# One-hot tiles of a routing table: two of six per batch moved from GpSimd to ScalarE

## The chip, the cores and the metric

The kernel runs on one core of a Trainium2 chip. The metric is the device time of one execution in microseconds (us). One execution was also profiled; its trace gives each instruction's start and length on TensorE (PE, with its weight loads as PEld), VectorE (DVE), ScalarE (ACT), GpSimd (POOL) and SyncE (SP, which issues DMAs).

## The reference

Four batches of 768 tokens, 8 heads of 64. First a chunked attention: each chunk of 32 queries sees 8 memory keys and a window of its neighbours. Its output, 3072 tokens of 512, goes to a top-1 mixture of 8 experts.

```python
def _moe_ref(x, modality_id, w_gate, modality_bias, w1, w2):
    logits = x @ w_gate + modality_bias[modality_id]
    e_idx = np.argmax(logits, axis=1)
    ...
    gate_w = probs[np.arange(N), e_idx]
    for e in range(E):
        mask = e_idx == e
        ...
        h = np.maximum(x[mask] @ w1[e], 0.0)
        out[mask] = gate_w[mask, None] * (h @ w2[e])
```

## The kernel before, in words

The attention is a loop over 32 half units (a unit is two heads of one batch, a half is 384 of its 768 tokens; variable `i`). One round of the loop issues: the score matmuls of half i (`scores`, line 339), the transposes and the exponential of half i-1 (`exps_t`, lines 357 on PE and 359 on ACT, tile `PT`), the maximum and the subtraction of half i on DVE (`less_max`, 347 and 350), then in even rounds the key transposes of the next unit and their copies (`trans_k`, `store_k`, line 331, three on ACT and one on DVE), in odd rounds Pool's copies of shared value rows (`share_v`, line 289) and the query transposes (`trans_q`, line 303; `store_q`, line 308 on ACT); then the second product of half i-1 (`attend`, line 369, which needs `PT`), the transposes of half i-2 (`trans_x`, line 391 on PE, copied by ACT in line 394) and the normalisation of half i-1 on DVE (`normalize`, lines 377 to 384).

When the four units of a batch are done, a generator `route(b)` finds each token's expert and its rank in the expert's list, and writes the token's number into a table, 128 rows by 192 columns. The table is built by six matmuls (line 663), one per 128 tokens: the stationary tile `l1` is a one-hot of the low part of the rank (128 wide, tile `l` in the trace), the moving tile `a1` is a one-hot of expert and high part times the token's number (192 wide, tile `a`). `lo` and `ac` are the numbers that the one-hots are made from; both are ready well before. The table of the first three batches is read by the first `gather` (line 720), which opens the expert stage.

The generator's steps are fed into the attention loop by `pump(k)`, which issues the next k steps, each of which ends with a `yield "v"`. There are calls of `pump` in each round: one after the maximum, one after the subtraction, three and three around `store_k` (the second three behind the three copies on ACT), three inside and after `normalize`, one at the round's end. The batch before the last takes three times as many.

Each engine runs its queue in order. PE, SP and Pool run in the order in which the program issues. ACT and DVE do so too, but only up to round 26 (`MAN = 26`); from there to the end of the attention a planner orders these two by its own costs. Batches 0 and 1 are routed before round 26, batch 2 around rounds 25 to 29, batch 3 behind the loop, where the expert stage already runs.

Of the kernel before, what the change touches and what calls it, by code (L numbers as in the profile page):

```python
# [15 lines left out]
ALU = mybir.AluOpType  # L16
# [4 lines left out]
P = 128  # L21
B, H, S, D = 4, 8, 768, 64
NMEM = 8
NCH = S // 32
NT = S // P
# [11 lines left out]
ROW_X = ROW_R1 + 1  # L37
ROW_L = 32
NEARLY = 3
NPOOL = 2  # L40
NP3 = 0
NACT = 2
CPOOL = (10, 12, 13, 14, 15)
MAN = 26
# [8 lines left out]
def tile_chunk_attention_top1_moe(  # L53
# [14 lines left out]
    nc = tc.nc  # L68
# [22 lines left out]
    def bank():  # L91
        return ps.tile([P, 512], F32, name="tr", tag="tr", bufs=4)
# [72 lines left out]
    iota = const.tile([P, 192], F32, name="iota")  # L165
# [4 lines left out]
    tokm = const.tile([P, N // P], F32, name="tokm")  # L170
# [352 lines left out]
    def route(b):  # L523
# [72 lines left out]
        lo = sm.tile([P, NT, 1], F32, name="lo")  # L596
        nc.vector.scalar_tensor_tensor(lo[:, :, 0], hi[:, :, 0], -float(P), rank[:, :, 0], op0=ALU.mult, op1=ALU.add)
        yield "v"
        ac = sm.tile([P, NT, 1], F32, name="ac")
# [39 lines left out]
        for t in range(NT):  # L639
            l1 = rt.tile([P, P], F32R, name="l1", bufs=NT)  # L640
            a1 = rt.tile([P, 192], F32R, name="a1", bufs=NT)
            T = b * NT + t
            if b == B - 1 and NP3 <= t < NP3 + NACT:
                dist = sm.tile([P, 192], F32, name="dist", bufs=2)
                nc.scalar.activation(dist[:, 0:P], iota[:, 0:P], AF.Abs, scale=-1.0, bias=lo[:, t])
                nc.scalar.activation(l1, dist[:, 0:P], AF.Relu, scale=-1.0, bias=1.0)
                dist = sm.tile([P, 192], F32, name="dist", bufs=2)
                nc.scalar.activation(dist, iota, AF.Abs, scale=-1.0, bias=ac[:, t])
                nc.scalar.activation(a1, dist, AF.Relu, scale=tokn[:, T:T + 1], bias=tokm[:, T:T + 1])
                hot.append((l1, a1))  # L650
                continue
            eng = nc.gpsimd if t < (NPOOL, NPOOL, NPOOL, NP3)[b] else nc.vector
            eng.tensor_scalar(l1, iota[:, 0:P], lo[:, t], None, op0=ALU.is_equal)
            yield "v"
            eng.tensor_scalar(a1, iota, ac[:, t], tokm[:, T:T + 1], op0=ALU.is_equal, op1=ALU.mult)
            yield "v"
            hot.append((l1, a1))
        if b == B - 1:
# [171 lines left out]
    t = bank()  # L830
# [23 lines left out]
    for i in range(n + 2):  # L854
# [53 lines left out]
        if i >= 2:  # L908
            u2, hf2 = units[i - 2]
            if hf2 == 1 and u2 % 4 == 3:  # L910
                routing.append((route(u2 // 4), True, u2 // 4, 0))
# [186 lines left out]
```

## Time and profile before

| | |
|---|---|
| timed runs | 453.59 us median of 3 (453.19 to 454.4) |
| profiled execution | 455.18 us, of which 453.4 us from first to last instruction |
| busy PE, DVE, ACT, POOL | 425.5, 310.5, 261.6, 195.8 us |
| mean granted TensorE clock | 0.984 of full |

The span falls in two stages: the attention up to about 145 us, and the expert stage behind it. An engine's busy share says little by itself; what counts is which wait ends last at a place. "Idle" in brackets in the rows is the time that an engine stood still before an instruction, with what released it.

### The profile page before, as it was taken

What the parts mean: (1) busy time and instruction counts of PE and PEld (TensorE: products, weight loads), DVE (VectorE), ACT (ScalarE), POOL (GpSimd) and SP (SyncE); (2) the same over time, 40 slices, a digit from 0 to 9 for tenths busy, and PEclk for the clock granted to TensorE, in tenths of its full rate; (3) what the DMA queues carried; (4) which work ended last, traced back from release to release, by engine and by line L of the source; (5) the groups of instructions that cost most, each with busy time, mean ns of one, the idle gap of its engine ahead of it and who ended that gap; (6) DMA issues with size and microseconds to landing.
All of it is one profiled execution on the core that took longest, in us unless ns stands there. A gap on an engine that the chain in (4) does not pass through costs nothing. (4 is left out here: it accounts for less than half of the span.)

```text
span 453.4 us, 11700 instructions
## 1 busy us (share of the span) xinstructions
PE 425.5 (94%) x4009; PEld 359.0 (79%) x4009; DVE 310.5 (68%) x746; ACT 261.6 (58%) x524; POOL 195.8 (43%) x373
## 2 busy tenths in 40 slices
PE   7879999999977998999999999999999999999993
PEld 4658787776856787989796977989898988898982
DVE  7888799797877699848465454757666574848430
ACT  5747776675636664747366455656565655657421
POOL 8867679579798932214051211303040404040201
PEclk9989999999979999999999999999999999999997
DMA  6899999999977502177196834202662201111101
GB/s 185 149 227 205 220 218 205 207 209 198 220 180 213 192 3 93 54 227 226 38 261 208 225 97 142 90 0 95 180 210 76 90 5 50 47 49 48 46 2 46
DMA packets 74818, 61.66 MB, mean 136 GB/s; under 512 B 36091, under 2 KB 64979, under 8 KB 74740
## 3 DMA queue, kind: packets, MB, share of 16 engines
q1 hardware_dynamic: 68000, 41.50, 40.2%
q0 software_dynamic: 5888, 19.11, 13.8%
q8 instruction: 36, 0.59, 0.6%
q14 instruction: 42, 0.34, 0.3%
q10 hardware_dynamic: 852, 0.11, 0.2%
HBM read 77.43 MB, written 12.76 MB: 199 GB/s over the span
## 5 line engine op out<-in xcount | busy, mean ns | idle before, releaser
L760 PEld LDWEIGHTS tr<-xt,w 128*128 128x128 f32 x1152 | 141.0, 189 | 4.9 <-issue 2.6
L760 PE MATMUL tr<-xt,w 128*128 128x256 f32 (+1 forms) x1152 | 142.9, 284 | 1.8 <-PEq L1059 0.6
L770 PE MATMUL av<-wh,h 128*128 128x512 f32 x384 | 128.4, 400 | 0.0
L795 POOL DMA_INDIRECT out_dram<-o,ix_now x24 | 24.2, 1008 | 157.1 <-ACT o L791 156.2
L764 DVE SCALAR_TENSOR_TENSOR h<-tr,h 128x256 fp32r<-128x256 f32 x96 | 40.6, 423 | 70.8 <-ACT h L761 53.1
L770 PEld LDWEIGHTS av<-wh,h 128*128 128x128 f32 x384 | 72.2, 188 | 17.3 <-issue 1.7
L770 PE MATMUL av<-wl,h 128*128 128x512 f32 x192 | 75.8, 395 | 0.0
L289 POOL COPY vw<-vw 24x384 f32<-24x384 f32 (+1 forms) x128 | 61.1, 515 | 24.5 <-DMA vw<-in_v_dram 23.2
L708 DVE TENSOR_TENSOR wl<-raw,wh 128x512 fp32r<-128x512 f32 x91 | 63.0, 692 | 8.1 <-ACT wh L706 0.8
L761 ACT ACTIVATE h<-tr 128x256 fp32r<-128x256 f32 x96 | 36.8, 385 | 51.8 <-PE tr L760 32.7
L708 DVE TENSOR_TENSOR w<-raw,w 128x512 fp32r<-128x512 f32 x93 | 60.4, 694 | 8.4 <-ACT w L706 8.4
L706 ACT CAST wh<-raw 128x512 fp32r<-128x512 f32 x96 | 58.8, 614 | 1.3 <-DMA raw<-in_moe_w_dram 1.3
L706 ACT CAST w<-raw 128x512 fp32r<-128x512 f32 x96 | 53.8, 622 | 0.0
L791 ACT ACTIVATE o<-av,gate_now 128x512 f32<-128x512 f32 x24 | 16.2, 689 | 46.3 <-PE av L770 37.3
L770 PEld LDWEIGHTS av<-wl,h 128*128 128x128 f32 x192 | 36.2, 188 | 7.1
L331 ACT COPY kbd<-tr 64x672 f32<-64x672 f32 x47 | 36.5, 777 | 6.4 <-PE tr L325 5.5
L369 PE MATMUL av<-vw,PT 128*32 128x130 f32 x768 | 29.3, 286 | 3.7 <-ACT PT L359 1.8
L359 ACT ACTIVATE PT<-tr 128x384 f32<-128x384 f32 x32 | 15.8, 492 | 28.6 <-PE tr L357 28.1
L339 PE MATMUL sc<-kbd,qT 128*32 128x128 f32 x768 | 29.3, 289 | 1.9 <-POOL kbd L313 1.9
L723 POOL DMA_INDIRECT xg<-xd,gx x24 | 26.5, 1105 | 9.8 <-POOL gx L721 6.2
L369 PEld LDWEIGHTS av<-vw,PT 128*32 128x32 f32 x768 | 20.5, 113 | 9.3 <-ACT PT L359 4.3
L743 ACT CAST xt<-tr 128x512 fp32r<-128x512 f32 x24 | 13.9, 586 | 23.0 <-PE tr L741 13.4
(237 smaller groups left out, 524.5 us busy)
## 6 DMA issues: line engine op xcount, KB each, us to landing
raw<-in_moe_w_dram SPq DMA_DIRECT2D x192, 256.0 KB
k<-in_k_dram SPq DMA_DIRECT2D x16, 384.0 KB
q<-in_q_dram SPq DMA_DIRECT2D x16, 384.0 KB
xd<-xb POOLq DMA_DIRECT2D x16, 384.0 KB, 6.0
vw<-in_v_dram SPq DMA_DIRECT2D x32, 184.0 KB
vw<-in_mem_v_dram SPq DMA_DIRECT2D x32, 48.0 KB
vw<-in_v_dram SPq DMA_DIRECT2D x32, 6.0 KB
vw<-in_v_dram SPq DMA_DIRECT2D x32, 2.0 KB
```

Of the source, the lines that this page charges most:

```text
L289: nc.gpsimd.tensor_copy(vw[r0:r0 + 24, c + 1:c + 1 + w, h, 0:D], vw[r0 + 32:r0 + 56, c:c + w, h, 0:D])
L331: copy(dst.rearrange("p c (i j) -> p c i j", j=2)[:, :, :, j], win)
L339: nc.tensor.matmul(sc[32 * j:32 * j + 32, t * P:(t + 1) * P], qT[:, 32 * c:32 * c + 32], kbd[:, c].rearrange("p h m -> p (h m)"), start=Tr ...
L369: nc.tensor.matmul(avb[32 * j:32 * j + 32, t * W:(t + 1) * W], PT[:, t * P + 32 * j:t * P + 32 * j + 32], vw[:, c].rearrange("p h d -> p ( ...
L706: nc.scalar.copy(wh[i], raw[i])
L708: (eng or nc.vector).tensor_sub(wl[i][:, s], raw[i][:, s], wh[i][:, s].bitcast(F32))
L723: nc.gpsimd.indirect_dma_start(out=xg[t], out_offset=None, in_=xd[0:rows], in_offset=bass.IndirectOffsetOnAxis(ap=gx[:, t:t + 1], axis=0))
L760: nc.tensor.matmul(pw, wt[f][:, c * P:(c + 1) * P], x[:, c, 0:w], start=(n == 0), stop=(n == 11))
L761: nc.scalar.activation(hh[:, f], ph, AF.Relu)
L764: nc.vector.scalar_tensor_tensor(hl[:, f], ph, 0.0, hh[:, f].bitcast(F32), op0=ALU.max, op1=ALU.subtract)
L770: nc.tensor.matmul(pos[t], x, w[8 + f], start=(f == 0 and n == 0), stop=(f == 7 and n == 2))
L795: nc.gpsimd.indirect_dma_start(out=out, out_offset=bass.IndirectOffsetOnAxis(ap=ix_now[:, t:t + 1], axis=0), in_=outs[t], in_offset=None, ...
```

## The change

Before, of the six pairs of one-hot tiles of each of the first three batches, the first two were made by Pool (two instructions a pair) and the last four by DVE. Now the first four are made by DVE and the last two by ACT, in the way that two pairs of the last batch were made already: the absolute distance to the wanted column, then a rectifier that leaves 1 (or the token's number) at distance 0 and 0 elsewhere, so four instructions a pair. Two `yield "v"` are put among those, so a pair counts two steps of the pump as the others do. In the last batch the same pairs stay on the same engines.

```diff
-NPOOL = 2
-NP3 = 0
 NACT = 2
...
-            if b == B - 1 and NP3 <= t < NP3 + NACT:
+            if (t < NACT) if b == B - 1 else (t >= NT - NACT):
                 dist = sm.tile([P, 192], F32, name="dist", bufs=2)
                 nc.scalar.activation(dist[:, 0:P], iota[:, 0:P], AF.Abs, scale=-1.0, bias=lo[:, t])
                 nc.scalar.activation(l1, dist[:, 0:P], AF.Relu, scale=-1.0, bias=1.0)
+                yield "v"
                 dist = sm.tile([P, 192], F32, name="dist", bufs=2)
                 nc.scalar.activation(dist, iota, AF.Abs, scale=-1.0, bias=ac[:, t])
                 nc.scalar.activation(a1, dist, AF.Relu, scale=tokn[:, T:T + 1], bias=tokm[:, T:T + 1])
+                yield "v"
                 hot.append((l1, a1))
                 continue
-            eng = nc.gpsimd if t < (NPOOL, NPOOL, NPOOL, NP3)[b] else nc.vector
-            eng.tensor_scalar(l1, iota[:, 0:P], lo[:, t], None, op0=ALU.is_equal)
-            yield "v"
-            eng.tensor_scalar(a1, iota, ac[:, t], tokm[:, T:T + 1], op0=ALU.is_equal, op1=ALU.mult)
+            nc.vector.tensor_scalar(l1, iota[:, 0:P], lo[:, t], None, op0=ALU.is_equal)
+            yield "v"
+            nc.vector.tensor_scalar(a1, iota, ac[:, t], tokm[:, T:T + 1], op0=ALU.is_equal, op1=ALU.mult)
             yield "v"
             hot.append((l1, a1))
```

## Rows read from the trace of the kernel before

**Rows 1.** Stages: window, length, busy PE, PEld, DVE, ACT, POOL, clock, DMA share, GB/s

```profile
20.00:40.00 20.00, 16.25 (x253) 12.37 (x253) 16.95 (x54) 10.50 (x19) 15.62 (x33) 0.91 1.00 205
...
120.00:140.00 20.00, 16.07 (x250) 12.38 (x242) 15.14 (x58) 7.83 (x16) 16.57 (x29) 0.83 0.92 206
...
180.00:220.00 40.00, 40.00 (x266) 36.15 (x266) 28.94 (x53) 25.37 (x53) 10.27 (x19) 1.00 0.51 155
```

**Rows 2.** Tile dist: ns min/median/max of ACT's one-hot instructions, first and last start

```profile
L645 ACT ACTIVATE dist<-iota,lo x2: 387/396/404, 160.5 to 161.8; 128x128 f32<-128x128 f32 x2
L648 ACT ACTIVATE dist<-iota,ac x2: 441/442/442, 160.8 to 162.1; 128x192 f32<-128x192 f32 x2
L646 ACT ACTIVATE l<-dist x2: 294/294/295, 161.2 to 162.5; 128x128 fp32r<-128x128 f32 x2
L649 ACT ACTIVATE a<-dist,tokm,tokn x2: 532/533/534, 161.4 to 162.7; 128x192 fp32r<-128x192 f32 x2
```

**Rows 3.** Tiles l and a: one-hot instructions on DVE and POOL, same columns

```profile
L653 DVE TENSOR_SCALAR l<-iota,lo x16: 269/282/532, 67.0 to 163.3; 128x128 fp32r<-128x128 f32 x16
L653 POOL TENSOR_SCALAR l<-iota,lo x6: 594/608/692, 71.3 to 130.0; 128x128 fp32r<-128x128 f32 x6
...
L655 POOL TENSOR_SCALAR a<-iota,ac,tokm x6: 1003/1038/1097, 71.9 to 130.6; 128x192 fp32r<-128x192 f32 x6
```

**Rows 4.** Timeline of ACT, rounds 14 to 16: start, us, instruction, [idle before]

```profile
66.37 2.41 ACT L331 COPY kbd<-tr 64x672 f32<-64x672 f32 x3
68.80 0.48 ACT L394 COPY xT<-tr 128x384 f32<-128x384 f32 x1
69.36 0.49 ACT L359 ACTIVATE PT<-tr 128x384 f32<-128x384 f32 x1
...
72.41 0.48 ACT L394 COPY xT<-tr 128x384 f32<-128x384 f32 x1 [1.74 <-PE tr L391]
```

**Rows 5.** Timeline of PE, round 15

```profile
69.91 0.87 PE L369 MATMUL av<-vw,PT 128*32 128x130 f32 x24
71.86 0.52 PE L391 MATMUL tr<-ident,xb 128*128 128x128 f32 x3 [1.08 <-DVE xb L384]
```

**Rows 6.** Timelines of ACT and PE, batch 1 (rounds 23 and 24)

```profile
100.31 0.49 ACT L359 ACTIVATE PT<-tr 128x384 f32<-128x384 f32 x1
...
102.00 0.87 PE L369 MATMUL av<-vw,PT 128*32 128x130 f32 x24 [1.13 <-DMA k<-in_k_dram]
...
108.05 0.81 PE L663 MATMUL tr<-a,l 128*128 128x192 f32 x5 [1.10 <-POOL a L655]
```

**Rows 7.** Timeline of PE, batch 2 (rounds 29 and 30)

```profile
128.87 0.52 PE L391 MATMUL tr<-ident,xb 128*128 128x128 f32 x3 [1.47 <-DVE xb L384]
...
131.75 1.38 PE L663 MATMUL tr<-a,l 128*128 128x192 f32 x5 [1.28 <-POOL a L655]
133.07 1.51 PE L339 MATMUL sc<-kbd,qT 128*32 128x128 f32 x24
```

**Rows 8.** Timeline of DVE: round 14, then batch 2's first and last one-hot

```profile
65.94 0.56 DVE L350 TENSOR_TENSOR sb<-sc,mx 128x384 f32<-128x384 f32 x1
...
67.92 0.53 DVE L653 TENSOR_SCALAR l<-iota,lo 128x128 fp32r<-128x128 f32 x1
...
129.10 0.38 DVE L653 TENSOR_SCALAR l<-iota,lo 128x128 fp32r<-128x128 f32 x1
...
130.91 0.39 DVE L655 TENSOR_SCALAR a<-iota,ac,tokm 128x192 fp32r<-128x192 f32 x1
```

**Rows 9.** Timeline of POOL: copies of shared rows, and the first gather's index

```profile
64.84 3.92 POOL L289 COPY vw<-vw 24x384 f32<-24x384 f32 x8 [1.94 <-DMA vw<-in_v_dram]
...
131.76 3.64 POOL L289 COPY vw<-vw 24x384 f32<-24x384 f32 x8
...
136.31 0.18 POOL L720 CAST ix<-table 128x2 int32 x1
```

**Rows 10.** Timeline of PE, early in the attention

```profile
27.93 0.52 PE L321 MATMUL tr<-ident,k 128*128 128x128 f32 x3 [1.84 <-DMA k<-in_k_dram]
```

## The prediction

> **What bounds the kernel now.** I read the table of stages first, for where time lost on one engine is still there at the end. Between 180 and 220 us PE is busy all 40 of 40 us at a granted clock of 1.00 [rows 1]: the expert stage is a chain of matmuls, so a shift of its start is a shift of the end, and the question is when the attention hands over. The attention is where the change acts. There I went through the timelines of PE, ACT, DVE and Pool around the three places where a table is made, looking for what PE waits for, since PE issues every round in order.
>
> The reader should see three things. First, PE does wait for Pool's one-hots: 1.10 us before the table matmuls of batch 1 [rows 6] and 1.28 us before those of batch 2 [rows 7]; in batch 0 no such wait is worth naming. Second, ACT has free time in a round, but not everywhere: in round 14 it makes three key copies from 66.37 on, then the copy of line 394 at 68.80, then the exponential of the next half at 69.36, with no idle between them, and its idle 1.74 us come only before 72.41 [rows 4]. PE's second product starts at 69.91, right behind that exponential [rows 5]. Third, PE has two stretches at the lower of its two clocks: a mean of 0.91 over 20 to 40 us is 3.6 us at 1.2 instead of 2.4 GHz (0.09 x 20 x 2), and 0.83 over 120 to 140 us is 6.8 us [rows 1].
>
> **What leaves Pool.** Two pairs per batch, a median of 0.61 and 1.04 us a tile [rows 3]: 2 x 1.65 = 3.3 us per batch. That is worth what PE waited for it. In batch 1 the 1.10 us idle before the table matmuls go, and the five late matmuls no longer start together: I take -1.2 us. In batch 2 DVE's own four pairs end at 130.91 + 0.39 = 131.30 [rows 8], only 0.45 us before Pool's release at 131.75 [rows 7]. But with DVE's pairs first in the order of the matmuls, most of the six are done by then, instead of one, and scores that now start at 133.07 [rows 7] could start near 131.9: -1.2 us again, with 0 and -1.6 as its bounds. Pool's copies of shared rows for the last unit, at 131.76 now [rows 9], and the first gather behind them at 136.31, move forward by up to 3.3 us. I count nothing for it, because the gathered rows are transposed only behind the last second products of the attention, which PE reaches no earlier for it; a lower bound of -0.5 us.
>
> **What DVE does.** The same number of pairs, four a batch, but four steps of the pump earlier: the pairs take the slots right behind the normalisation and around the next maximum. In round 14 the subtraction that starts at 65.94 [rows 8] then stands behind three more one-hots, at up to 0.53 us each [rows 3], and ends near 68.1 instead of 66.5. What it feeds, the exponential at 69.36 [rows 4], is later than that, so this is hidden; without that cover it would cost those 1.6 us once a batch.
>
> **What ACT gets.** Eight instructions per batch. By their medians a pair is 0.396 + 0.294 + 0.442 + 0.532 = 1.66 us, two pairs 3.3 us; in the last batch, where a planner interleaves them, the second pair starts 1.3 us behind the first [rows 2], so 2.6 us is the lower bound and 3.3 the upper. In batches 0 and 1 ACT runs in issue order, each rectifier right behind the distance that it reads, so I take 3.0. No table of functions is at stake: the last batch already runs both functions here between exponentials.
>
> Where they fall decides. I count the twelve steps. Four go where Pool's four went. Three (DVE's fifth to seventh) go ahead of `store_k`. The three calls behind `store_k` take DVE's eighth tile and then the first ACT pair: behind the copies at 66.37 and before line 394. The last two steps, the second ACT pair, go into `normalize`, behind line 394 and before the next exponential [rows 4]. So both pairs stand in front of the exponential now at 69.36. Some 0.2 us of gap between 68.80 and 69.36 takes up a little: it starts 2.8 us later (2.4 to 3.1), near 72.2, and the second product behind it near 72.7 instead of 69.91 [rows 5]. PE has nothing else to issue. The wait of 1.08 us before line 391 at 71.86 [rows 5] is DVE's and is over by then, so it is swallowed: net 2.8 - 1.1 = +1.7 us.
>
> Batch 1 repeats it: the exponential at 100.31 is pushed, and behind it stands a second product that already waits 1.13 us for data with a pace of its own [rows 6]. Net again +1.7 us. Both together +3.4 (bounds 2 x 1.3 and 2 x 2.0). In batch 2 ACT's order is the planner's; its pairs need only be ready when DVE's are, at 131.3, so I count nothing, with the 1.3 us of a batch as the upper bound.
>
> **The clock.** A wait of 1.84 us before 27.93 [rows 10], with shorter ones ahead of it, comes before the low stretch of 3.6 us, and waits of 1.47 and 1.28 us close together before that of 6.8 us [rows 1, 7]; single waits of 1.08, 1.13 and 1.10 us [rows 5, 6] were not followed by one. The two new ones last 2.8 us each and have the length that is followed by 1.2 GHz. If each brings 3.6 us of it and PE is the bound there, half of that is lost, up to 1.8 us; I take 1.5 each, +3.0, with 0 and 6.8/2 = 3.4 us each as ends. On the other side the second low stretch of today may not come, as one of its two waits shrinks: up to -3.4, probably -2 if it comes to that, and I take half, -1.0.
>
> The Trainium skill speaks against the change at another place: its GPSIMD Engine Reference, section 8, says that Pool shares its SBUF interfaces with VectorE, so the two contend in some of VectorE's modes. The trace agrees so far that DVE's 128-wide one-hot takes from 269 to 532 ns [rows 3], and 0.53 us at 67.92 [rows 8] under Pool's copies, which run from 64.84 for 3.92 us [rows 9]. By the rule a freed Pool starts its next copies under DVE's one-hots.
>
> **The sum** for the profiled execution (455.18 us): -1.2 - 1.2 + 3.4 + 3.0 - 1.0 = +3.0, so 458.2. That execution was 1.6 us above the median of 453.59; against the median it is 456.6 us.
>
> **Rivals.** (B) The same stops, but the clock does not fall behind them, or the low stretch of batch 2 goes whole: +3.4 - 2.4 = +1.0, less up to 2 when both help. For it: after 1.08 to 1.13 us nothing happened. Against: these are more than twice as long. 452.6 to 455.0 us, middle 454.2. (C) Faster: ACT's pairs are hidden. If they push the exponential by no more than the 1.1 us that PE waits there anyway, the stops cost nothing and the two table waits go: -2.4 us, 451.2, with the low stretch gone too 449. It decides at 1.1 us per batch; against it stands that ACT has no idle time between 66.37 and 69.85 [rows 4] and the least insertion is 2.6 us. It would need ACT to run in another order than issue. (D) The table waits stay: Pool's last copies, 3.3 us earlier, run under DVE's one-hots of batch 2, and a tile takes up to 0.25 us more (0.532 less 0.282 [rows 3], taken for both widths), eight tiles 2.0, so that the last is ready at 133.3 and not at today's 131.75: +1.5 instead of -1.2 there. For it: the 0.53 at 67.92 against 0.38 at 129.10 [rows 8]. Against: when ACT has already delayed PE and DVE, but not Pool, whose copies follow the loads, the two miss each other. 453.6 + 3.0 + 2.7 = 459.3 us.
>
> **How the numbers follow.** My forecast has 0.55, B 0.27, C 0.13, D 0.05. The forecast's own range is 455 to 459. The range that leaves out C and the far tails of the others (under 2 in 10) is 452.4 to 459.2. A measurement of this kernel can tell about 0.3%, 1.36 us, from no change. Faster by more: nearly all of C and a tail of B, 0.13. Within: most of B and a little of the forecast, 0.27. Slower: the rest, 0.60.
>
> **What would show it.** Right: in rounds 15 and 23 PE stands still for 2.5 to 3 us before line 369, released by the exponential; ACT's lines 645 to 649 lie between the key copies and that exponential; the granted clock falls to half soon after at least one of them; no wait for one-hots before line 663 in batch 1; and the attention ends 1 to 5 us later. Wrong: ACT's eight instructions lie elsewhere, or PE's wait at line 369 is near 1 us, or the loads, which fill the DMA share to 1.00 early on [rows 1], set the pace so that a late PE catches up at the next data wait; or the low stretch between 120 and 140 us is gone and outweighs the rest.

## The result, and the profile after

The changed kernel is slower: 457.82 us median of 13 executions (454.7 to 459.8) against 454.40 for the kernel before on the same chip (13 executions, 452.57 to 456.2), a ratio of 1.0070, 95% interval 1.0043 to 1.0097. In us that is +3.2 (2.0 to 4.4); forecast was +3.0. Medians are over all executions; ratios, here and below, leave out slow ones, more than 1.5% above the fastest of the same kernel (so e6's rests on 7 of 12), and the profile of e5 is of such a one (461.54 us), so its rounds 15 to 25 are left out of the table below. The profiled execution of the changed kernel took 456.68 us, its span is 454.9 at a mean granted clock of 0.984, the same clock as before. In the changed kernel's line numbers everything stands one or two lower: 369 is 367, 391 is 389, 339 is 337, 331 is 329, 359 is 357, 394 is 392, 384 is 382, 663 is 662.

The stages of the kernel after, with the columns of [rows 1]:

```profile
60.00:80.00 20.00, 17.34 (x292) 13.66 (x292) 16.67 (x48) 14.66 (x29) 13.75 (x28) 0.91 1.12 208
100.00:120.00 20.00, 17.57 (x280) 13.12 (x283) 15.21 (x39) 14.24 (x29) 13.51 (x27) 0.91 1.18 210
120.00:140.00 20.00, 16.27 (x310) 12.86 (x302) 17.78 (x66) 12.68 (x28) 12.13 (x24) 1.00 0.60 146
180.00:220.00 40.00, 40.00 (x271) 36.40 (x270) 29.32 (x59) 24.77 (x51) 11.79 (x20) 1.00 0.53 162
```

And two stages of the kernel before that [rows 1] does not have:

```profile
60.00:80.00 20.00, 18.92 (x349) 15.01 (x345) 18.70 (x55) 13.93 (x26) 17.44 (x33) 1.00 1.15 209
100.00:120.00 20.00, 17.76 (x304) 13.93 (x306) 15.72 (x43) 12.33 (x24) 17.97 (x35) 1.00 1.15 219
```

The clock, third from the right, now has a low stretch in each of the two stages in which the tables of batches 0 and 1 are made, where it had none; between 120 and 140 us it is 1.00 instead of 0.83. The expert stage is as full as it was (40 of 40 us), so what is lost ahead of it stays lost: from the first matmul on an expert's weights to the end it takes 307.6 us (before 307.9), and 307.6 to 308.8 in the experiments below except e3 (310.5).

ACT in rounds 14 and 15 of the kernel after, where [rows 4] has the copies, line 394 and the exponential with no idle between them:

```profile
65.73 2.39 ACT L329 COPY kbd<-tr 64x672 f32<-64x672 f32 x3
68.02 0.39 ACT L643 ACTIVATE dist<-iota,lo 128x128 f32<-128x128 f32 x1
...
69.69 0.48 ACT L392 COPY xT<-tr 128x384 f32<-128x384 f32 x1
...
71.19 0.55 ACT L648 ACTIVATE a<-dist,tokm,tokn 128x192 fp32r<-128x192 f32 x1
71.64 0.47 ACT L357 ACTIVATE PT<-tr 128x384 f32<-128x384 f32 x1
...
74.56 0.48 ACT L392 COPY xT<-tr 128x384 f32<-128x384 f32 x1 [1.66 <-PE tr L389]
```

Both pairs stand ahead of the exponential, one on each side of the copy of line 392. From the key copies to the exponential are 71.64 - 65.73 = 5.91 us; before, 69.36 - 66.37 = 2.99 [rows 4]. That is 2.9 us more. ACT's idle time, 1.66 us, comes behind, as before.

PE in the kernel after, in batch 0, batch 1 and batch 2 (compare [rows 5], [rows 6] and [rows 7]):

```profile
69.90 0.55 PE L301 MATMUL tr<-ident,qr 128*128 128x128 f32 x3 [0.94 <-DVE kbd L329]
72.16 1.53 PE L367 MATMUL av<-vw,PT 128*32 128x130 f32 x24 [1.72 <-ACT PT L357]
73.62 0.90 PE L389 MATMUL tr<-ident,xb 128*128 128x128 f32 x3
74.45 1.18 PE L337 MATMUL sc<-kbd,qT 128*32 128x128 f32 x24
...
104.50 0.55 PE L301 MATMUL tr<-ident,qr 128*128 128x128 f32 x3 [1.00 <-DMA vw<-in_v_dram]
...
106.20 1.53 PE L367 MATMUL av<-vw,PT 128*32 128x130 f32 x24 [1.15 <-ACT PT L357]
...
112.19 0.89 PE L662 MATMUL tr<-a,l 128*128 128x192 f32 x6
...
134.80 0.52 PE L389 MATMUL tr<-ident,xb 128*128 128x128 f32 x3 [2.61 <-ACT a L648]
135.25 0.87 PE L367 MATMUL av<-vw,PT 128*32 128x130 f32 x24
136.05 0.91 PE L662 MATMUL tr<-a,l 128*128 128x192 f32 x6
```

In round 15 PE stands still for 0.94 + 1.72 = 2.66 us ahead of the second product, and that product then takes 1.53 us instead of 0.87. The wait that [rows 5] has behind it (1.08 us for xb) is swallowed. Round 23 repeats it with 1.00 + 1.15 us. The wait for the table's one-hots in batch 1, 1.10 us in [rows 6], is gone: line 662 starts with no idle before it. In batch 2 the wait for one-hots is gone as well, but the one ahead of line 389, 1.47 us in [rows 7], is now 2.61. The releaser named there had long been done; what ended it was xb, as the rows of VectorE further down show.

PE's clock around the stop of round 15, in windows of 1 us:

```profile
71.00:72.00 1.00, 0.00 (x0) 0.00 (x0) 0.97 (x3) 0.97 (x3) 0.66 (x1) 0.87 1.24 133
72.00:73.00 1.00, 0.84 (x16) 0.79 (x20) 0.32 (x1) 0.90 (x3) 0.00 (x0) 0.50 1.10 183
...
74.00:75.00 1.00, 1.00 (x15) 0.63 (x17) 0.71 (x2) 0.44 (x1) 1.00 (x3) 0.50 0.80 136
75.00:76.00 1.00, 1.00 (x24) 0.78 (x17) 0.29 (x1) 0.04 (x1) 0.94 (x3) 0.92 0.94 213
```

0.50 is 1.2 instead of 2.4 GHz. The means of the first and last window put the fall at 71.74 us, still in the stop, and the rise at 75.16: 3.4 us, of which PE works 3.0.

### The profile page after: what moved, and what is told of

Same layout as the page of the kernel before. It is cut to its first block, busy times and chain, and to the rows that moved or that the text cites. A ratio compares the mean times of both kernels' runs of the same rounds, so it can differ in the third digit from the quotient of the medians.

```text
span 454.9 us, 11703 instructions
## 1 busy us (share of the span) xinstructions
PE 425.7 (94%) x4009; PEld 358.0 (79%) x4009; DVE 312.0 (69%) x746; ACT 269.6 (59%) x548; POOL 186.2 (41%) x361
## 5 line engine op out<-in xcount | busy, mean ns | idle before, releaser
L287 POOL COPY vw<-vw 24x384 f32<-24x384 f32 (+1 forms) x128 | 59.8, 505 | 30.2 <-DMA vw<-in_v_dram 29.1
L722 POOL DMA_INDIRECT xg<-xd,gx x24 | 27.5, 1144 | 10.2 <-POOL gx L720 6.6
```

The costliest lines, as they stand in the source:

```text
L287: nc.gpsimd.tensor_copy(vw[r0:r0 + 24, c + 1:c + 1 + w, h, 0:D], vw[r0 + 32:r0 + 56, c:c + w, h, 0:D])
L722: nc.gpsimd.indirect_dma_start(out=xg[t], out_offset=None, in_=xd[0:rows], in_offset=bass.IndirectOffsetOnAxis(ap=gx[:, t:t + 1], axis=0))
```

## The experiments

A good measure from one profile is the time between the first score matmuls of two rounds, since what comes before round 15 (67.9 us before, 65.6 to 71.8 in the experiments, though nothing differs there) drops out of it. Rounds 15 to 25 hold what the change does in batches 0 and 1, rounds 29 to 30 its place in batch 2. Each ratio is to the kernel before on the same chip, where that had 454.25 to 455.64 us.

| kernel | pairs by ACT: batches 0, 1 | batch 2 | us | ratio (95%) | 15 to 25 | 29 to 30 |
|---|---|---|---|---|---|---|
| before | none (Pool first) | none (Pool first) | | 1 | 40.87 | 8.28 |
| after | last | last | 457.82 | 1.0070 (1.0043-1.0097) | 45.72 | 7.42 |
| e1 | last | none | 458.08 | 1.0075 (1.0042-1.0108) | 45.75 | 7.40 |
| e2 | none | last | 456.73 | 1.0035 (1.0000-1.0069) | 40.08 | 9.73 |
| e3 | last, filler on PE | last | 457.68 | 1.0068 (1.0033-1.0103) | 43.03 | 10.73 |
| e4 | last, issued later | last | 456.99 | 1.0057 (1.0025-1.0089) | 40.84 | 9.50 |
| e5 | none | first | 453.53 | 0.9979 (0.9951-1.0008) | | 6.93 |
| e6 | first, issued later | none | 454.07 | 0.9958 (0.9920-0.9997) | 41.17 | 7.72 |
| e7 | first, issued later | first | 451.90 | 0.9944 (0.9916-0.9973) | 40.00 | 8.28 |
| e8 | none | none (Pool last) | 454.50 | 0.9958 (0.9925-0.9991) | 39.45 | 9.51 |
| e9 | last, issued later | first | 453.75 | 0.9964 (0.9932-0.9995) | 40.99 | 6.84 |
| e10 | as e2 | | 454.82 | 0.9993 (0.9960-1.0026) | 40.76 | 10.13 |
| e11 | as e5 | | 453.60 | 0.9971 (0.9942-1.0000) | 41.21 | 8.18 |
| e12 | as e8 | | 454.32 | 0.9999 (0.9973-1.0026) | 40.63 | 8.61 |

e1 to e4 shared a chip, as did e5 to e7, e8 and e9, and e10 to e12. "First" and "last" are the first and the last two of the six pairs. Where the last two are not VectorE's, its eight one-hots stand four steps earlier than before; below they are called early. Six kernels have the code of before in batches 0 and 1 and a value for rounds 15 to 25 (before, e2, e8, e10, e11, e12): 39.45 to 41.21 us, 40.50 on average. That is the scatter against which one profile has to be read.

**e1 and e2: the change in two halves.** The first makes it in batches 0 and 1 alone, the second in batch 2 alone; elsewhere Pool makes its two pairs as before.

```diff
-            if (t < NACT) if b == B - 1 else (t >= NT - NACT):
+            if (t < NACT) if b == B - 1 else (b < B - 2 and t >= NT - NACT):  # e1
+            if (t < NACT) if b == B - 1 else (b == B - 2 and t >= NT - NACT):  # e2
...
+            eng = nc.gpsimd if b == B - 2 and t < 2 else nc.vector  # e1; e2: b < B - 2
```

> The change in batches 0 and 1 alone; batch 2 has its first two pairs on Pool as before. If the cost is ScalarE's place in front of the exponential in those two batches (theory), nothing of the gain of batch 2 is left and the kernel is about 4 us slower than before (two stops of 1.7 net, two low stretches of the clock of about 1.5, less 1.2 at the table matmuls of batch 1): 457 to 460 us against 454.4, ratio 1.007 to 1.012, slower than the whole change. If the cost lies in batch 2 (Pool's earlier copies under VectorE's one-hots), it is at or below the time before: ratio 0.996 to 1.001.

> The change in batch 2 alone; batches 0 and 1 have their first two pairs on Pool as before. Theory: the table wait shrinks and the low stretch of the clock behind it often stays away, so 1 to 3 us faster than before, ratio 0.993 to 0.998. Rival (the cost lies in batch 2): slower than before by 2 to 3 us, ratio 1.004 to 1.008.

Batches 0 and 1 alone are as slow as the whole change: 1.0075 against 1.0070, and the same 45.7 us for rounds 15 to 25. Batch 2 alone was expected to be faster and is not. In its profile PE waits 3.50 us ahead of the transposes of xb, where it waited 1.47 before. In time, e2 at 1.0035 lies between the theory (to 0.998) and the rival (from 1.004).

**e3: filler in the stops.** Six matmuls of 512 columns ahead of the second product in rounds 15 and 23, so that PE has 1.46 us of work inside each stop. It leaves the chain of waits as it is.

```diff
+        if now[0] in (15, 23):
+            for _ in range(6):
+                nc.tensor.matmul(avb, idle[:, 0:P], idle[:, P:640], start=True, stop=True)
```

> The whole change, and TensorE gets six matmuls of 512 columns whose result is overwritten, right before the second product of rounds 15 and 23, where it stands still: about 1.3 us of work inside each stop. They change no result. If a good part of the cost is the low clock behind the stops (theory), it stays at full clock there and the kernel is 2 to 3 us faster than the changed one, near the time before: ratio 0.999 to 1.002. If the clock there is a bystander, the fillers gain nothing and the ratio stays at 1.006 to 1.009.

PE of e3 in round 15:

```profile
68.96 1.46 PE L367 MATMUL av<-idle 128*128 128x512 bf16 x6
71.03 0.87 PE L371 MATMUL av<-vw,PT 128*32 128x130 f32 x24 [0.61 <-ACT PT L358]
...
72.31 0.86 PE L338 MATMUL sc<-kbd,qT 128*32 128x128 f32 x24
```

The second product takes 0.87 us again: no half clock. This splits the loss. From round 15 to 16 the kernel before takes 72.30 - 67.92 = 4.38 us, after 74.45 - 67.29 = 7.16, e3 72.31 - 66.16 = 6.15. So the stop costs 6.15 - 4.38 = 1.77 us and the clock behind it 7.16 - 6.15 = 1.01. Rounds 23 to 24 give 4.41, 7.17 and 6.16: 1.75 and 1.01. The whole time did not get shorter: 1.0068, where the theory had 0.999 to 1.002 and the rival 1.006 to 1.009. So the 1.01 us are shown for these two rounds alone. Rounds 15 to 25 are 2.7 us shorter than in the kernel after (43.03 against 45.72), but this profile loses more than that behind them: PE waits 4.34 us ahead of the transposes of xb in batch 2 and has the low clock there instead (rounds 29 to 30 10.73 us).

**e4: the same pairs, issued later.** ACT's pairs of batches 0 and 1 are held back and issued behind the query copies (line 306) of the next odd round, so behind the exponential.

```diff
+                if b < B - 2:
+                    act_later.append(pair)
+                else:
+                    pair()
...
             store_q(u + 1, 1)
+            while act_later:
+                act_later.pop(0)()
             pump(5)
```

> The whole change, but in batches 0 and 1 ScalarE's two pairs are issued one round later, behind the query copies (after the exponential that they stood in front of), where ScalarE had 1.7 us idle. Same instructions on the same engines. Theory: no stop before the second product of rounds 15 and 23, no low clock there; the exponential of the round after is pushed by 0.5 us at most; table waits stay gone: 2 to 4 us faster than before, ratio 0.991 to 0.997. If it is the amount of work on ScalarE that costs, or the freed Pool, and not the place: ratio 1.004 to 1.008 as for the change.

ACT of e4 in round 15:

```profile
69.29 0.49 ACT L357 ACTIVATE PT<-tr 128x384 f32<-128x384 f32 x1 [0.38 <-PE tr L355]
69.99 0.93 ACT L306 COPY qT<-tr 128x384 f32<-128x384 f32 x2 [0.21 <-PE tr L301]
70.78 0.42 ACT L644 ACTIVATE dist<-iota,lo 128x128 f32<-128x128 f32 x1
...
73.93 0.46 ACT L392 COPY xT<-tr 128x384 f32<-128x384 f32 x1
```

The eight instructions now lie where ACT was idle, between the query copies and the copy of line 392. Rounds 15 to 25 are back at 40.84 us (before 40.87), with VectorE's four earlier steps still in place, so in these two batches those steps are hidden, as forecast. The time went against it: 1.0057, where 0.991 to 0.997 was expected, and within the 1.004 to 1.008 of the rival. In batch 2 PE waits 3.57 us for xb. That made the second theory: in batch 2 VectorE's earlier one-hots get ahead of the normalisation.

**e5 to e7: VectorE's order as before.** ACT makes the first two pairs instead of the last two, so VectorE's eight one-hots keep the places that they had behind Pool's. e5 does so in batch 2 alone, e6 in batches 0 and 1 alone (issued later, as in e4), e7 in all three.

```diff
-            if (t < NACT) if b == B - 1 else (t >= NT - NACT):
+            if t < NACT:  # e7
+            if (t < NACT) if b == B - 1 else (b == B - 2 and t < NACT):  # e5; e6: b < B - 2
```

> The change in batch 2 alone, but ScalarE makes the first two pairs there, so that VectorE's eight one-hots keep the places they have in the kernel before, behind the normalisation; batches 0 and 1 as before, with Pool's pairs. Theory (in batch 2 the cost is VectorE's order: one-hots four steps earlier stand ahead of the normalisation): the wait of PE ahead of the transposes of xb goes back from 3.5 to about 1.5 us, the table's wait of 1.28 us stays away or shrinks below 0.5, and the time is 0.995 to 1.000 of before, at least 0.3% under the kernel with the last two pairs in batch 2 alone (1.0035). Rival (ScalarE's two pairs themselves, or the gather that Pool is now free for, cost the time in batch 2): the wait stays at 2.5 us or more or moves to the exponential, and the time is 1.003 to 1.006 of before.

> ScalarE instead of Pool in batches 0 and 1 alone, with the first two pairs, issued behind the query copies of the next round, and VectorE's one-hots at the places they have in the kernel before; batch 2 as before, with Pool's pairs. Theory (in batches 0 and 1 only the place of ScalarE's pairs ahead of the exponential costs): no stop of 2 us or more ahead of the scores of rounds 15 and 23, no half clock there, the table's wait of batch 1 (1.10 us) gone, so rounds 15 to 25 in 39.8 to 40.9 us (before 40.87) and the time 0.996 to 1.000 of before. Rival (VectorE's share or the work that ScalarE does in these rounds costs wherever it stands): rounds 15 to 25 in 42 us or more and 1.003 or more of before.

> Both cures together, in all three batches: ScalarE makes the first two pairs, in batches 0 and 1 behind the query copies of the next round, and VectorE's one-hots keep the places of before. Theory (two located costs, the place of ScalarE's pairs in batches 0 and 1 and VectorE's order in batch 2): both gone and the table's waits of batches 1 and 2 (1.10 and 1.28 us) with them, 0.993 to 0.998 of before, the fastest of all. Rival (the work costs wherever it stands, or the gains are lost to the next wait): 0.999 to 1.006 of before.

All three came out about where the theory put them; only rounds 15 to 25 of e6 took 0.3 us more than expected (41.17), and PE waits 1.97 and 1.87 us for xb there. e7 is faster than the kernel before: 0.9944, 2.5 us less (1.2 to 3.8). It ran on one chip only, and two other kernels moved by 0.4% from one chip to another (e10 and e12 below). PE of e7 in round 15 and at the table of batch 1:

```profile
70.81 0.55 PE L389 MATMUL tr<-ident,xb 128*128 128x128 f32 x3 [1.15 <-DVE xb L382]
...
105.99 0.89 PE L667 MATMUL tr<-a,l 128*128 128x192 f32 x6
```

The wait of 1.08 us of [rows 5] is there again (1.15), nothing waits for the exponential, and the wait for the table of batch 1 is gone.

**e8 and e9: the order alone, and the mixture.** e8 is the kernel before, except that in batch 2 Pool makes the last two pairs; ACT makes none. e9 is e4 with ACT's first pairs in batch 2.

```diff
-            eng = nc.gpsimd if t < (NPOOL, NPOOL, NPOOL, NP3)[b] else nc.vector
+            eng = nc.gpsimd if (t >= NT - NPOOL if b == B - 2 else t < (NPOOL, NPOOL, NPOOL, NP3)[b]) else nc.vector  # e8
...
-            if (t < NACT) if b == B - 1 else (t >= NT - NACT):
+            if (t >= NT - NACT) if b < B - 2 else (t < NACT):  # e9
```

> The kernel before with one edit in batch 2: Pool makes the last two pairs instead of the first two, so VectorE's eight one-hots move up four steps; ScalarE makes none. Theory (in batch 2 the cost is VectorE's order): VectorE's one-hots again run ahead of the normalisation, PE's wait ahead of the transposes of xb is 2.5 us or more, although ScalarE has nothing to do with it; the time is 1.002 to 1.010 of before, since Pool's pairs also come later. Rival (ScalarE's pairs, or the Pool that they free, cost the time in batch 2): that wait is 1.0 to 1.6 us as before, whatever the table's wait is.

> As in the change, VectorE makes the first four pairs and ScalarE the last two in batches 0 and 1, but ScalarE's are issued behind the query copies of the next round; in batch 2 ScalarE makes the first two pairs. It differs from the kernel with all first pairs (0.9944) in VectorE's four earlier steps in batches 0 and 1, and from the kernel with the late pairs alone (1.0057) in the order of batch 2. Theory (the earlier steps are hidden in batches 0 and 1, and cost only in batch 2): 0.992 to 0.998 of before, rounds 15 to 25 in 39.8 to 41.0 us, PE's wait ahead of the transposes of xb in batch 2 at 1.0 to 1.6 us. Rival (VectorE's earlier steps cost in batches 0 and 1 too): 1.000 to 1.005 of before.

PE of e8 at the table of batch 1, which is as in the kernel before, and in batch 2:

```profile
104.20 0.89 PE L663 MATMUL tr<-a,l 128*128 128x192 f32 x6
...
126.75 0.87 PE L391 MATMUL tr<-ident,xb 128*128 128x128 f32 x3 [3.09 <-DVE xb L384]
```

e8 has the stop (3.09 us ahead of the transposes of xb), so VectorE's order makes it and ACT has nothing to do with it. In all seven profiles with early one-hots in batch 2 this wait is 2.61 to 4.34 us, in the seven others 1.11 to 1.97. But its price was missed: 0.9958 where 1.002 to 1.010 was expected. e9 is at 0.9964, as the theory had it, with a wait of 1.97 us for xb, over the 1.6 expected.

**e10 to e12: batch 2 once more, on one chip.** The kernels of e2, e5 and e8, unchanged, because the 0.6 to 0.9% between e2 or e4 and the rest lay between chips.

> The change in batch 2 alone, once more, now beside its two relatives on one chip: VectorE's one-hots early, ScalarE's pairs last. Theory (VectorE's early one-hots together with ScalarE's late pairs cost time in batch 2): 1.002 to 1.006 of before, at least 0.4% above both relatives. Rival (the 0.6% between this kernel and its relatives lay in the chips on which they ran, and batch 2 decides nothing): all three within 0.3% of one another, at 0.996 to 1.000 of before.

> ScalarE's pairs first and VectorE's one-hots behind the normalisation, in batch 2 alone, once more. Theory (order in batch 2): 0.996 to 1.000 of before, PE's wait ahead of the transposes of xb 1.0 to 1.6 us. Rival (chips): as the other two, within 0.3%.

> Pool's pairs last and VectorE's one-hots early, in batch 2 alone, once more; it shares VectorE's order with the first of these three and not ScalarE's work. If VectorE's order alone has a price, it stands with the first, at 1.002 to 1.006; if the price needs ScalarE's late pairs or Pool's copies under VectorE's one-hots too, it stands with the second, at 0.994 to 1.000, although PE's stop ahead of the transposes of xb is again near 3.1 us.

Side by side e2's kernel is at 0.9993, not at 1.0035, and all three lie within 0.3%, as the rival had it. The waits do repeat, 3.40, 1.92 and 3.28 us ahead of the transposes of xb, though e11's 1.92 is over the 1.6 expected. VectorE of e10 in batch 2, then its PE, then its Pool:

```profile
126.41 0.37 DVE L653 TENSOR_SCALAR l<-iota,lo 128x128 fp32r<-128x128 f32 x1
...
127.68 0.17 DVE L375 TENSOR_SCALAR den<-av 128x6 f32<-128x6 f32 x1
...
128.53 0.52 DVE L653 TENSOR_SCALAR l<-iota,lo 128x128 fp32r<-128x128 f32 x1
128.97 0.18 DVE L377 RECIPROCAL den<-den 128x6 f32<-128x6 f32 x1
...
129.40 0.54 DVE L382 TENSOR_TENSOR xb<-av,den 128x384 f32<-128x384 f32 x1
```

```profile
130.09 0.87 PE L389 MATMUL tr<-ident,xb 128*128 128x128 f32 x3 [3.40 <-DVE xb L382]
```

```profile
127.55 3.69 POOL L287 COPY vw<-vw 24x384 f32<-24x384 f32 x8
```

VectorE of e11, the same place:

```profile
128.16 0.17 DVE L375 TENSOR_SCALAR den<-av 128x6 f32<-128x6 f32 x1
128.35 0.19 DVE L377 RECIPROCAL den<-den 128x6 f32<-128x6 f32 x1
...
128.90 0.55 DVE L382 TENSOR_TENSOR xb<-av,den 128x384 f32<-128x384 f32 x1
129.82 0.58 DVE L653 TENSOR_SCALAR l<-iota,lo 128x128 fp32r<-128x128 f32 x1
```

In e10 one-hots begin 1.3 us ahead of den, fill the time between den and its reciprocal, and xb starts 1.72 us behind den (129.40 - 127.68). In e11 xb starts 0.74 us behind den and the one-hots follow. The kernel after has e10's order:

```profile
131.92 0.27 DVE L652 TENSOR_SCALAR l<-iota,lo 128x128 fp32r<-128x128 f32 x1
...
132.99 0.16 DVE L375 TENSOR_SCALAR den<-av 128x6 f32<-128x6 f32 x1
...
134.10 0.55 DVE L382 TENSOR_TENSOR xb<-av,den 128x384 f32<-128x384 f32 x1
```

Its Pool stands still meanwhile, from 131.08 us on, until that xb can be stored:

```profile
134.95 0.83 POOL L394 DMA_DIRECT2D xd<-xb  x1 [3.87 <-DVE xb L382]
```

Over all profiles, rounds 29 to 30 take 7.42 to 10.73 us in the seven with VectorE's early one-hots (mean 9.38) and 6.84 to 8.28 in the seven others (mean 7.66): 1.7 us. About half of that is made up again before the expert stage: from round 25 to the first matmul on an expert's weights the seven take 34.33 to 38.72 us (mean 36.72), the others 34.72 to 36.95 (mean 35.84), 0.9 us apart. In whole times as little is left: e2, e8, e10 and e12, which change batch 2 alone to early one-hots, average 0.9996, e5 and e11 0.9975. A difference of 0.2%, about 1 us, is within their intervals.

## Why the prediction was right, and where it was not

**What bounds the kernel**: right. The loss is made by waits in the attention, and the expert stage gives none of it back (307.6 us against 307.9).

**The table waits** (-1.2 us in batch 1): the wait is gone, but its price was read from one execution. Rounds 24 to 25 went from 5.51 to 4.52 us, -0.99. In the six profiles in which Pool makes this table's first pairs, the wait is 1.10 us (before), 0.77 (e10) and 0.41 (e11), and is not there in e2, e8 and e12; rounds 24 to 25 take 4.16 to 5.51 us, 4.73 on average. With ACT's pairs and PE at full clock (e3, e4, e6, e7, e9) they take 4.15 to 4.16. So the gain is about 0.6 us on average.

**ACT's place** (+1.7 us in each of batches 0 and 1): right. The pairs lie where the count of steps put them, the exponential is 2.9 us later (forecast 2.8), PE stands still 2.66 us in round 15 and 2.15 in round 23 (forecast 2.5 to 3), and net of the swallowed wait the stop costs 1.77 and 1.75 us (e3), 3.5 together (forecast 3.4). That it is the place and not the work is shown by rounds 15 to 25 of e4, e6, e7 and e9: with the same eight instructions behind the query copies they take 40.00 to 41.17 us, as without them (39.45 to 41.21). The 0.94 us released by DVE's key copy, which the prediction did not have, lies inside the same stop, whose end the exponential sets; it is absent in e4 and e9, with the same order on VectorE.

**The clock** (+1.5 for each stop): right in kind, too large. The clock fell behind both stops, which rival B denied, and cost 1.01 us each, 2.0 and not 3.0. The stretch is as long as assumed (3.4 us for 3.6), but part of it lies in the stop, and of the 3.0 us that PE works in it about a third is lost, not half. The whole time of e3 does not show this price.

**Batch 2** (-1.2 for the table's wait, -1.0 for the clock): this is the step that failed. "What DVE does" took the four earlier steps as hidden, from round 14 of batch 0, where that held, and applied it to all three batches. In batch 2 the pump is three times as fast and a planner orders VectorE (no run separates the two); there the one-hots got ahead of den, reciprocal and xb, and PE waits for xb. Pool's late one-hots no longer hold the table up, but one stop of 2.6 to 4.3 us stands in place of two waits of 1.47 + 1.28 = 2.75 [rows 7]. So batch 2 gained nothing: +1.6 us in e2, -0.3 in e10, where -2.2 was forecast. Behind this stop the low clock came in e2, e3, e4, e8, e10 and e12, but not in the profile of the kernel after. It came in batch 2 of e1, e6, e7 and e11 too, so it is not tied to the early order.

**The sum.** Measured in profiles, batches 0 and 1 are -1.0 + 3.5 + 2.0 = +4.5 us against the forecast's +5.2 (-1.2 + 3.4 + 3.0); rounds 15 to 25 show +4.85 against the one profile of before, and +5.2 against the mean of the six (40.50). Timed, e1 has +3.4 (1.9 to 4.9). The one profiled execution is only 1.5 us above that of before (458.2 was forecast, 456.68 came), in a spread of 5 us between executions: its +4.85 are offset by -2.3 from round 25 to the first matmul on an expert's weights (36.67 before, 34.33 after), -0.6 before round 15 and -0.4 behind. These -2.3 look like the -2.2 forecast for batch 2, but one profile does not show that: with the code of before in batch 2 the same stretch takes 35.09 in e1 and 35.20 in e6, and with the change's order 36.91 to 38.72 in e2, e3, e4 and e10.

That the total came out as forecast is in part luck: by the times, batches 0 and 1 cost less than forecast (+3.4 for +5.2) and batch 2 brought nothing instead of -2.2, and the two errors cancel. Of the 1.4 us between e1's rounds and its time the cause stays open; the stretch from round 25 on varies by more than that between profiles of equal code (36.67 before, 35.09 in e1).

**Rivals.** B has a second condition, that the low stretch of batch 2 goes whole. In the one profile of the kernel after it did (1.00 from 120 to 140 us), and that execution lies between B's 454.2 and the forecast's 458.2. C, the faster one, gave 451.2 us and said that it needs ACT to run in another order than issue; e7 issues ACT's pairs in such an order, and makes other pairs on ACT, and takes 451.9. D's mechanism was seen in part: VectorE's one-hot took 0.27 us at 131.92 in the kernel after, when Pool had no work, and 0.52 at 128.53 in e10 under Pool's copies. The Trainium skill (GPSIMD Engine Reference, section 8) says that Pool shares SBUF interfaces with VectorE and that the two contend in some of VectorE's modes. The two times agree with that. But what the longer one-hots delay is xb and not the table, and in the kernel after Pool's copies had ended.

What stays open: what VectorE's early order in batch 2 costs in the whole time (0.2% by the averages, not resolved), and why e2's kernel and e8's moved by 0.4% from one chip to another; e4 (1.0057) against e9 (0.9964) may hold the same.

## What to carry to other kernels

When work moves to an engine with idle time, look where in its queue it lands: the same 3 us cost 1.8 us and the clock behind it ahead of the exponential, and nothing that rounds 15 to 25 show behind the query copies. A wait read from one profile is one draw: the 1.10 us of batch 1's table came in one of six profiles and was shorter or missing in the other five. An engine that keeps its number of instructions but makes other tiles of a list changes its own order, and that has to be followed at every place where the list is made, above all where another scheduler takes over. A difference of half a per cent between kernels that ran on different chips is not yet a result: put them side by side on one.

## What the runs showed of the hardware that was not expected

The length of a stop alone did not tell whether the clock would fall behind it. Behind 0.94 + 1.72 us in round 15 it fell (0.50 for 3.4 us), and behind 1.92 us in batch 2 of e11 and 1.43 us in batch 2 of e7; behind 2.61 us in batch 2 of the kernel after it did not (1.00), nor behind 1.97 and 1.87 us in rounds 15 and 23 of e6. Matmuls of 512 columns in the stop kept it up in e3 (1.00 from 60 to 80 and from 100 to 120 us). One stage of e11, two windows of e7 and two stages of e6, the clock third from the right:

```profile
120.00:140.00 20.00, 16.42 (x252) 12.47 (x246) 16.30 (x57) 10.50 (x25) 13.22 (x25) 0.83 0.95 217
```

```profile
128.00:129.00 1.00, 0.88 (x7) 0.58 (x11) 1.00 (x3) 1.00 (x4) 0.99 (x3) 0.61 1.27 280
129.00:130.00 1.00, 1.00 (x24) 0.84 (x22) 1.00 (x4) 0.47 (x2) 0.94 (x3) 0.50 0.70 179
```

```profile
60.00:80.00 20.00, 18.03 (x329) 14.77 (x328) 19.34 (x53) 16.52 (x32) 15.07 (x30) 1.00 1.15 223
100.00:120.00 20.00, 18.13 (x320) 14.09 (x309) 16.92 (x46) 15.96 (x31) 13.80 (x28) 1.00 1.08 206
```
